# Attention and expert kernel on one core: q, k, v by one 128-partition transfer per tensor and batch, and row scatters no longer ordered among themselves

## The chip, the cores and the metric

The kernel runs on one core of one Trainium2 chip. The metric is device time in microseconds (us): the median of 3 runs is 343.91 us (343.42 to 345.1). One more execution was profiled, and its rows are shown below.

Engines are named as in the profile: PE (matmul), PEld (its weight loads), DVE (VectorE), ACT (ScalarE), POOL (GpSimd), SP (which here only issues loads). Each executes its own instructions in a fixed order, and waits at an instruction until what that one needs is there.

## What is computed

Linear attention over 8 batches of 8 heads, 576 positions and head size 64 gives rows x of 512 numbers, 4608 of them. Each row is then sent to one of 8 experts (512 to 1024 to 512), and its result is scaled by its gate weight.

```python
q_s = exp(q - max(q)) / sum           # over the head size
k_s = exp(k - max(k)) / sum           # over the positions
kv  = einsum('bhsd,bhse->bhde', k_s, v)
x   = einsum('bhsd,bhde->bhse', q_s, kv)   # (4608, 512) after a transpose
logits = x @ w_gate + modality_bias[modality_id]
e_idx, gate_w = argmax(logits), softmax(logits)[e_idx]
out[row] = gate_w * (relu(x[row] @ w1[e]) @ w2[e])   # e = e_idx[row]
```

The kernel first assumes that each of the two modalities has one expert (slot 0 and slot 1, read from the bias on the chip) and computes those two. A loop behind it, `For_i(0, nr)`, does all experts over again for the rows when that assumption fails; in these runs it has no round.

## The kernel before

**Attention, batch by batch.** `load_batch(b)` loads k, v and q (1.18 MB each, fp32) into staging tiles `st`. They come from a pool of 5 buffers, in turn, so that a load waits until the tile five before it has been consumed. `ek` and `eq` (exp on ACT) and `vb` (a cast on POOL, two pieces a batch) are what consumes them. The 576 positions are spread as 64 partitions by 9, so a head fills 64 partitions; the 4 heads 0 to 3 lie on partitions 0 to 63, the heads 4 to 7 on partitions 64 to 127, each half by a transfer of its own.

`stage_a(b)` goes in a chain: `kv_ps` (PE, 36 matmuls), `kinv` and `kvbd` (DVE), `tp_ps` (transposes of `eq`), `et`, `kvT`, `g_ps`, `lg_ps` (PE), then some 30 small DVE operations for logits, the expert and the position of each row (`qi` to `hlo`), and `hv` on POOL. `scl` holds the factors of the rows. `stage_b(b)` makes x in five tiles (`x_ps` on PE, `x_sb` on DVE), sorts the rows by expert with a permutation matmul (`xT_ps`) and writes them on ACT and DVE into `xs`, from the left for slot 0, from the right for slot 1. `id_ps` and `lst` collect where each row goes.

**Experts.** After every second batch, one pass of 512 rows of each slot is complete and `ffn` computes it: 32 matmuls `h_ps`, relu to `hT` (ACT and DVE), 32 matmuls `y_ps`, four copies to `y_sb` (pool `ybuf`, 4 buffers), and for each copy one indirect DMA of POOL that scatters 128 rows of `out`. Eight passes have 512 rows, the last two 384: 608 matmuls, 38 scatters. Three pairs of passes belong to batches 1, 3 and 5; the last four passes (224 matmuls) can begin only after batch 7. The weights of the two slots come by eight 1 MB loads through the same staging tiles and are cast to `W`.

**What sets the order.** A scheduler places the instructions of each engine in one static order, from its own model of dependencies and durations; attention has priority (`high_priority(offset=AHEAD)`), and expert work fills in. It also takes all writes to `out` as one dependency, so each scatter waits for the completion of the one before it. Loads and scatters signal on 8 semaphores each, in turn: a DMA also waits for the one that used its semaphore before.

Of the kernel before, what the change touches and what calls it, by code (L numbers as in the profile page):

```python
# [16 lines left out]
ALU = mybir.AluOpType  # L17
# [3 lines left out]
P = 128  # L21
# [21 lines left out]
def kernel(  # L43
# [12 lines left out]
    nc = tc.nc  # L56
    B, H, S, Dh = q.shape
# [6 lines left out]
    NT = 5  # L64
# [31 lines left out]
    def load_batch(b):  # L96
        for nm, src in (("k", k), ("v", v), ("q", q)):
            t = stage.tile([P, HG, NJ * Dh], FP32, name="st", tag="st")
            for hg in range(2):
                nc.sync.dma_start(  # L100
                    out=t[64 * hg : 64 * hg + 64],
                    in_=bass.AP(
                        tensor=src.tensor,
                        offset=src.offset + (b * H + hg * HG) * S * Dh,
                        ap=[[NJ * Dh, 64], [S * Dh, HG], [1, NJ * Dh]],
                    ),
                )
            st[nm, b] = t
# [6 lines left out]
    wg_f = const.tile([P, KD, E], FP32)  # L115
    nc.scalar.dma_start(out=wg_f, in_=moe_w_gate.rearrange("(kp p) e -> p kp e", p=P))
    mraw = const.tile([P, B, NJ, 2], I32)
# [160 lines left out]
    def stage_a(b):  # L278
# [69 lines left out]
        for t in range(NT):  # L348
# [44 lines left out]
        scl = small.tile([P, NT, H], FP32, name="scl")  # L393
        nc.vector.tensor_tensor(
            out=scl, in0=view(qi, [[H, NT], [1, H]]), in1=view(gsum, [[1, NT], [0, H]]), op=ALU.mult
        )
        na = small.tile([P, NT], FP32, name="na")
# [64 lines left out]
    def stage_b(b):  # L462
# [85 lines left out]

    def ffn(lo, w, slot, ix):
        hT = hbuf.tile([P, KF, GW], BF16, name="hT")  # L550
# [14 lines left out]
        for t in range(w // P):  # L565
            y_ps = ff.tile([P, D], FP32, name="y_ps", tag="ff")
            for kf in range(KF):
                nc.tensor.matmul(  # L568
                    out=y_ps,
                    lhsT=hT[:, kf, t * P : (t + 1) * P],  # L570
                    rhs=W[:, slot, W2 + kf * D : W2 + (kf + 1) * D],
                    start=(kf == 0),
                    stop=(kf == KF - 1),
                )
            y_sb = ybuf.tile([P, D], FP32, name="y_sb")
            if t % 4 < 3:
# [4 lines left out]
            nc.gpsimd.indirect_dma_start(  # L581
                out=out,
                out_offset=bass.IndirectOffsetOnAxis(ap=ix[:, c : c + 1], axis=0),
                in_=y_sb,
                in_offset=None,
                bounds_check=N - 1,
                oob_is_err=False,
            )

    eids = nc.values_load_multi_w_load_instructions(  # L590
        eid_i[0:1, 0:2],
# [6 lines left out]
    for b in range(B):  # L598
# [11 lines left out]
        if b % 2:  # L610
# [8 lines left out]
            for slot, (_, lo, w) in todo:  # L619
                ffn(lo, w, slot, idx)  # L620

# [33 lines left out]
    with tc.For_i(0, nr) as e:  # L655
        kcol = small.tile([P, 1], FP32, name="kcol")
        nc.vector.tensor_copy(out=kcol, in_=view(wrow, [[1, 1]], e))
        sel1 = small.tile([P, NSL], FP32, name="sel1")
# [7 lines left out]
        for _, lo, w in passes_a + passes_b:  # L666
            ffn(lo, w, 0, ixe)

# [29 lines left out]
```

## Time and profile before

| | before |
|---|---|
| median of 3 runs | 343.91 us |
| profiled execution | 346.28 us, span 344.6 us |
| busy: PE, DVE, ACT, POOL | 219.9, 174.6, 116.2, 75.7 us |
| scatters on POOL | 38, busy 37.3 us, idle ahead of them 138.9 us |
| loads of k, v, q | 28.3 MB, issued by SP, 48 transfers |

The span is the time from the first to the last instruction in the profile. Busy time of an engine is an average over stages that have different limits, so the rows further below are taken stage by stage. Durations of matmuls are modelled ends of pipelined work.

### The profile page before, as it was taken

The numbers are of one execution on the slowest core, as the hardware profiler recorded it, in microseconds if no ns is written. First come the engines' busy times: TensorE is split into PE (matmuls) and PEld (weight loads), VectorE is DVE, ScalarE is ACT, GpSimd is POOL, SyncE is SP. The second block draws the span as 40 slices with busy tenths as digits, with TensorE's granted clock in tenths as the row PEclk, the third lists the DMA queues.
The fourth block names the chain that finished last, engine by engine and source line by source line (L and its number), as shares of the span: only waits on it lengthen the run. The fifth ranks groups of instructions, "written<-read, shape, count | busy, mean of one in ns | idle before, by whom it ended". The sixth has DMA issues, their size and how long they took to land.

```text
span 344.6 us, 4646 instructions
## 1 busy us (share of the span) xinstructions
PE 219.9 (64%) x1637; PEld 126.0 (37%) x1657; DVE 174.6 (51%) x558; ACT 116.2 (34%) x161; POOL 75.7 (22%) x86
## 2 busy tenths in 40 slices
PE   0033373369994041572699997499799599999900
PEld 0023262234441031361554553364464334455400
DVE  4056856853520018639649668737858823123210
ACT  0324146144360081242554464332251331422200
POOL 8102100400111125420111433400322322232320
PEclk9999999999999555555589999569999969999985
DMA  7999977963799915999997612100010110212010
GB/s 146 215 222 221 345 233 149 261 242 122 153 233 239 243 70 129 241 208 212 173 213 165 148 55 82 62 1 2 30 60 36 50 71 30 93 61 91 26 69 6
DMA packets 21053, 46.60 MB, mean 135 GB/s; under 512 B 3360, under 2 KB 3360, under 8 KB 21025
## 3 DMA queue, kind: packets, MB, share of 16 engines
q1 hardware_dynamic: 16256, 36.70, 45.8%
q0 software_dynamic: 3040, 9.44, 7.4%
q10 hardware_dynamic: 1728, 0.10, 0.5%
q8 instruction: 15, 0.25, 0.3%
q14 instruction: 14, 0.11, 0.1%
HBM read 36.80 MB, written 9.96 MB: 136 GB/s over the span
## 4 chain that ended last, share of the span: by engine, by line
PE 16%; DMA 13%; issue 13%; DVE 6%; POOL 2%; ACT 1%; POOLq 0%; ACTq 0%
DMA out_dram<-y_sb,idx 13%; PE y_ps L568 5%; PE h_ps L554 4%; PE kv_ps L296 2%; PE xT_ps L494 2%; POOL hv L438 1%; DVE x_sb L486 1%; PE x_ps L478 1%; PE tp_ps L308 1%; PE id_ps L521 1%; ACT ek L284 1%; POOL out_dram L581 0%; PE lg_ps L350 0%; DVE hT L564 0%; DVE y_sb L577 0%
## 5 line engine op out<-in xcount | busy, mean ns | idle before, releaser
L554 PE MATMUL h_ps<-xs,W 128*128 128x512 bf16 (+1 forms) x307 | 76.8, 394 | 3.2 <-ACT xs L504 1.5
L568 PE MATMUL y_ps<-W,hT 128*128 128x512 bf16 x297 | 68.3, 379 | 1.3 <-DVE lo L428 0.7
L581 POOL DMA_INDIRECT out_dram<-y_sb,idx x38 | 37.3, 983 | 138.9 <-DMA out_dram<-y_sb,idx 61.0
L504 ACT CAST xs<-xT_ps 128x512 f32 (+2 forms) x40 | 21.9, 547 | 79.7 <-PE xT_ps L494 76.1
L562 ACT ACTIVATE hT<-h_ps 128x512 bf16<-128x512 f32 (+1 forms) x60 | 34.2, 578 | 39.1 <-PE h_ps L554 31.4
L554 PEld LDWEIGHTS <-W 128*128 128x128 bf16 x320 | 31.8, 103 | 35.7 <-issue 11.2
L568 PEld LDWEIGHTS <-hT 128*128 128x128 bf16 x304 | 29.1, 98 | 33.6 <-DVE hT L564 0.6
L494 PE MATMUL xT_ps<-perm,x_sb 128*128 128x128 bf16 (+1 forms) x160 | 20.8, 260 | 24.8 <-DVE x_sb L486 21.7
L577 DVE COPY y_sb<-y_ps 128x512 f32<-128x512 f32 x30 | 20.5, 687 | 28.2 <-PE y_ps L568 14.8
L486 DVE TENSOR_TENSOR x_sb<-x_ps,scl 128x512 bf16<-128x512 f32 (+1 forms) x40 | 27.4, 686 | 11.0 <-PE x_ps L478 10.8
L564 DVE TENSOR_SCALAR hT<-h_ps 128x512 bf16<-128x512 f32 (+1 forms) x20 | 13.1, 657 | 38.7 <-PE h_ps L554 38.6
L308 PE MATMUL tp_ps<-ident,eq 128*128 128x128 bf16 x144 | 15.5, 282 | 26.2 <-ACT eq L285 21.7
L438 POOL TENSOR_TENSOR hv<-hhi,vals 128x570 bf16<-128x570 bf16 x8 | 12.6, 1578 | 82.4 <-DVE hhi L434 82.4
L296 PE MATMUL kv_ps<-vb,ek 64*128 64x129 bf16 x288 | 18.5, 271 | 16.9 <-POOL vb L287 16.9
L505 DVE CAST xs<-xT_ps 128x512 f32 (+2 forms) x40 | 25.3, 633 | 4.9 <-ACT xs L504 4.6
L287 POOL CAST vb<-st 128x1152 bf16<-128x1152 f32 x16 | 18.6, 1187 | 37.0 <-DMA st<-in_v_dram 29.7
L494 PEld LDWEIGHTS <-x_sb 128*128 128x128 bf16 (+1 forms) x160 | 12.0, 114 | 35.6 <-DVE x_sb L486 31.7
L308 PEld LDWEIGHTS <-eq 128*128 128x128 bf16 x144 | 13.1, 130 | 30.5 <-ACT eq L285 22.4
L478 PE MATMUL x_ps<-kvbd,et 128*128 128x128 bf16 (+1 forms) x160 | 20.9, 271 | 2.7 <-ACT et L318 2.7
L296 PEld LDWEIGHTS <-ek 64*128 64x128 bf16 x288 | 15.7, 116 | 18.6 <-ACT ek L284 13.3
L285 ACT ACTIVATE eq<-st 128x2304 bf16<-128x2304 f32 x8 | 16.9, 2122 | 7.8 <-DMA st<-in_q_dram 7.8
L579 ACT COPY y_sb<-y_ps 128x512 f32<-128x512 f32 x8 | 4.7, 588 | 41.1 <-PE y_ps L568 21.1
(123 smaller groups left out, 210.1 us busy)
## 6 DMA issues: line engine op xcount, KB each, us to landing
st<-in_k_dram SPq DMA_DIRECT2D x16, 576.0 KB, 7.7
st<-in_v_dram SPq DMA_DIRECT2D x16, 576.0 KB, 10.8
st<-in_q_dram SPq DMA_DIRECT2D x16, 576.0 KB, 13.7
st<-in_moe_w_dram SPq DMA_DIRECT2D x8, 1024.0 KB, 12.6
out_dram<-y_sb,idx POOLq DMA_INDIRECT x38, 2.7
mraw<-in_moe_modality_id_dram ACTq DMA_DIRECT2D x2, 36.0 KB, 15.3
bias_b<-n_moe_modality_bias_dram ACTq DMA_DIRECT2D x1, 8.0 KB, 3.0
wg_f<-in_moe_w_gate_dram ACTq DMA_DIRECT2D x1, 16.0 KB
```

Of the source, the lines that this page charges most:

```text
L296: nc.tensor.matmul(out=kv[hg][:, 130 * hp : 130 * hp + 129], lhsT=ek[rows, j, P * hp : P * hp + P], rhs=vb[rows, j, hp, 0:129], start=(j = ...
L308: nc.tensor.transpose(out=view(tp, [[2 * nj * 64, 2], [1, 64]], hp * nj * 64 + jj * 64), in_=eq[:, c0 + jj, P * hp : P * hp + P], identity ...
L478: nc.tensor.matmul(out=x_ps[0:T, P * p_ : P * p_ + P], lhsT=et[:, p_, tcol[t] : tcol[t] + T], rhs=kvbd[:, p_, :], start=True, stop=True,)
L486: nc.vector.tensor_tensor(out=x_sb[0:T], in0=view(x_ps, [[Dh, H], [1, Dh]], 0, (0, T)), in1=view(scl, [[1, H], [0, Dh]], t * H, (0, T)), o ...
L494: nc.tensor.matmul(out=xT_ps[:, kd, 0:T], lhsT=view(x_sb, [[1, P]], kd * P, (0, T)), rhs=perm[0:T, t, 0:T], start=True, stop=True,)
L504: wa = nc.scalar.copy(out=window(a, passes_a[ph], T, ph == NPH - 1), in_=xT_ps[:, :, 0:T])
L505: wb = nc.vector.tensor_copy(out=window(a + right, passes_b[ph], T, ph == NPH - 1, True), in_=xT_ps[:, :, 0:T])
L554: nc.tensor.matmul(out=h_ps[:, 0:w], lhsT=W[:, slot, kd * F + f * P : kd * F + (f + 1) * P], rhs=xs[:, kd, lo : lo + w], start=(kd == 0), ...
L562: nc.scalar.activation(out=hT[:, f, 0:w], in_=h_ps[:, 0:w], func=ACT.Relu)
L568: nc.tensor.matmul(out=y_ps, lhsT=hT[:, kf, t * P : (t + 1) * P], rhs=W[:, slot, W2 + kf * D : W2 + (kf + 1) * D], start=(kf == 0), stop=( ...
L577: nc.vector.tensor_copy(out=y_sb, in_=y_ps)
L581: nc.gpsimd.indirect_dma_start(out=out, out_offset=bass.IndirectOffsetOnAxis(ap=ix[:, c : c + 1], axis=0), in_=y_sb, in_offset=None, bound ...
```

## The change

Each of k, v and q is loaded by one transfer over 128 partitions: even heads on partitions 0 to 63, odd heads on 64 to 127. What follows from the other order of heads: the gate weights `wg_f` come in four transfers instead of one, `scl` is written by two operations of half the size, and `x_ps` is written with the columns of the heads in their places. Scatters are declared independent of each other; only the loop behind waits for them.

```diff
-            for hg in range(2):
-                nc.sync.dma_start(
-                    out=t[64 * hg : 64 * hg + 64],
-                        offset=src.offset + (b * H + hg * HG) * S * Dh,
-                        ap=[[NJ * Dh, 64], [S * Dh, HG], [1, NJ * Dh]],
+            nc.sync.dma_start(
+                out=t,
+                    offset=src.offset + b * H * S * Dh,
+                    ap=[[NJ * Dh, P], [2 * S * Dh, HG], [1, NJ * Dh]],
...
-    nc.scalar.dma_start(out=wg_f, in_=moe_w_gate.rearrange("(kp p) e -> p kp e", p=P))
+    for h2 in range(2):
+        for hl in range(2):
+            nc.scalar.dma_start(
+                out=wg_f[64 * h2 : 64 * h2 + 64, 2 * hl : 2 * hl + 2, :],
...
+        for hl in range(2):
+            nc.vector.tensor_tensor(
+                out=view(scl, [[H, NT], [2, HG]], hl),
+                in0=view(qi, [[H, NT], [1, HG]], HG * hl),
...
-                    out=x_ps[0:T, P * p_ : P * p_ + P],
+                    out=view(x_ps, [[2 * Dh, 2], [1, Dh]], (4 * (p_ % 2) + p_ // 2) * Dh, (0, T)),
...
-            nc.gpsimd.indirect_dma_start(
+            store = nc.gpsimd.indirect_dma_start(
...
+            tc.declare_no_dep(store.ins, group=stores, reason="rows of their own")
+            tc.add_to_no_dep_group(stores, store.ins)
+            if stores == "stores":
+                stored.append(store)
...
+        for before in stored:
+            tc.add_manual_dep(first.ins, before.ins.name, ...)
```

The order of the built programs shows three places where instructions move.

**SP, start of the program.** SP's first loads of batch 0 and 1 before; DMAHW is a semaphore of a load, and "waits" names what must have landed first.

```order
L100 DMA st<-in_k_dram 64x4x576 x2
L100 DMA st<-in_v_dram 64x4x576 x2
L100 DMA st<-in_q_dram 64x4x576 [waits DMAHW0_49]
L100 DMA st<-in_q_dram 64x4x576 [waits DMAHW1_49]
L100 DMA st<-in_k_dram 64x4x576 [waits DMAHW2_49]
L100 DMA st<-in_k_dram 64x4x576 [waits DMAHW3_49]
```

And of the changed kernel, the same loads:

```order
L100 DMA st<-in_k_dram 128x4x576
L100 DMA st<-in_v_dram 128x4x576 [waits DMAHW0_49]
L100 DMA st<-in_q_dram 128x4x576 [waits DMAHW1_49]
L100 DMA st<-in_k_dram 128x4x576 [waits DMAHW2_49]
L100 DMA st<-in_v_dram 128x4x576 [waits DMAHW3_49]
L100 DMA st<-in_q_dram 128x4x576 [waits DMAHW4_49,Activation_49]
```

One row stands for two. The semaphores 0 to 3 belonged to `bias_b`, `wg_f` and the two `mraw` transfers; now they belong to `bias_b` and the first three of `wg_f`, so that v waits for `bias_b`, and the second k no longer for `mraw`.

**ACT, around batch 2.** Before, behind `ek` of batch 2: `hT` are the relus of the expert passes, `ek` here is that of batch 3, `eq` those of batches 2 and 3, and `et` belongs to the chain of batch 2.

```order
L562 ACTIVATE hT<-h_ps 128x512 x6
L272 CAST W<-st 128x2048
L579 COPY y_sb<-y_ps 128x512
L272 CAST W<-st 128x2048
L562 ACTIVATE hT<-h_ps 128x512 x6
L284 ACTIVATE ek<-st 128x4x9x64
L579 COPY y_sb<-y_ps 128x512
L285 ACTIVATE eq<-st 128x4x9x64 x2
L318 COPY et_180<-tp_ps 128x4x256
```

The changed kernel from `et` of batch 2 on; `eq` here is that of batch 3, `ek` that of batch 4, `kvT` and `lg` belong to batch 2:

```order
L328 COPY et_180<-tp_ps 128x4x256
L328 COPY et_180<-tp_ps 128x4x64
L349 COPY kvT<-kvT_ps 128x512
L576 ACTIVATE hT<-h_ps 128x512 x4
L295 ACTIVATE eq<-st 128x4x9x64
L387 ACTIVATE lg<-lg 128x40
L576 ACTIVATE hT<-h_ps 128x512
L294 ACTIVATE ek<-st 128x4x9x64
L481 TENSOR_LOAD aoff_i
```

Before, both expert passes of the first pair, with their 12 relus and the copies to `y_sb`, stood ahead of `eq` and `et` of batch 2; now `eq` of batch 2 stands in batch 1, and the relus are spread over batches 2 and 3, behind `et`. PE's order moved in the same way: before, 128 expert matmuls between batch 1 and the transposes of batch 2, now 49 to 73 in every batch from 2 to 7.

**POOL, the first scatters.** Before; DMASW is a semaphore of a scatter, `vb_183` is v of batch 3.

```order
L581 DMA out_dram<-y_sb,idx 4608x512 [waits DVE_49]
L581 DMA out_dram<-y_sb,idx 4608x512 [waits DMASW0_49,DVE_49]
L581 DMA out_dram<-y_sb,idx 4608x512 [waits DMASW1_49,DVE_49]
L581 DMA out_dram<-y_sb,idx 4608x512 [waits DMASW2_49,Activation_49]
L581 DMA out_dram<-y_sb,idx 4608x512 [waits DMASW3_49,DVE_49]
L581 DMA out_dram<-y_sb,idx 4608x512 [waits DMASW4_49,DVE_49]
L581 DMA out_dram<-y_sb,idx 4608x512 [waits DMASW5_49,DVE_49]
L287 CAST vb_183<-st 128x2x9x64 [waits DMAHW0_49,DMAHW7_49,PE_49,Pool_49]
```

And of the changed kernel, where `vb_183` is now v of batch 5:

```order
L452 TENSOR_TENSOR hv<-hhi,vals 128x570 [waits DVE_49]
L297 CAST vb_182<-st 128x2x9x64 [waits PE_49,Pool_49]
L595 DMA out_dram<-y_sb,idx 4608x512 [waits DVE_49] x3
L297 CAST vb_183<-st 128x2x9x64 [waits DMAHW7_49,PE_49,Pool_49]
L297 CAST vb_183<-st 128x2x9x64 [waits PE_49,Pool_49]
L595 DMA out_dram<-y_sb,idx 4608x512 [waits Activation_49]
```

The wait of each scatter for the one before it is gone (from the ninth on, one waits for the eighth before it), and the casts of `vb` for batches 3 and 4 stand ahead of the first scatter instead of behind the seventh and eighth.

## Rows read from the trace of the kernel before

**Rows 1.** Page, part 2: busy tenths in 40 slices of 8.6 us.
```profile
PE   0033373369994041572699997499799599999900
PEclk9999999999999555555589999569999969999985
DMA  7999977963799915999997612100010110212010
```

**Rows 2.** Windows: busy us of each engine, then PEclk, DMA share, GB/s.
```profile
22.00:34.00 12.00, 4.38 (x50) 3.37 (x50) 8.49 (x33) 5.05 (x5) 2.10 (x2) 1.00 1.05 221
38.00:46.00 8.00, 3.91 (x32) 2.79 (x29) 5.39 (x13) 2.02 (x5) 1.65 (x1) 1.00 1.03 393
```

**Rows 3.** Timeline, batches 0 and 1: start us, us, engine, instruction, [idle before <-releaser].
```profile
14.66 0.18 DVE L183 CAST modf<-mraw 64x32 f32<-64x32 int32 x1 [6.54 <-DMA mraw<-in_moe_modality_id_dram]
20.13 0.18 DVE L183 CAST modf<-mraw 64x32 f32<-64x32 int32 x1 [5.29 <-DMA mraw<-in_moe_modality_id_dram]
21.13 2.12 ACT L285 ACTIVATE eq<-st 128x2304 bf16<-128x2304 f32 x1 [7.85 <-DMA st<-in_q_dram]
26.25 0.21 DVE L322 TENSOR_SCALAR kinv<-kv_ps 128x2 f32<-128x2 f32 x2
...
49.27 0.26 DVE L322 TENSOR_SCALAR kinv<-kv_ps 128x2 f32<-128x2 f32 x2 [2.27 <-PE kv_ps L296]
```

**Rows 4.** Timeline of POOL: `hv` of batches 0 to 7.
```profile
40.56 1.65 POOL L438 TENSOR_TENSOR hv<-hhi,vals 128x570 bf16<-128x570 bf16 x1 [6.41 <-DVE hhi L434]
64.89 1.66 POOL L438 TENSOR_TENSOR hv<-hhi,vals 128x570 bf16<-128x570 bf16 x1 [22.68 <-DVE hhi L434]
137.64 1.14 POOL L438 TENSOR_TENSOR hv<-hhi,vals 128x570 bf16<-128x570 bf16 x1 [2.69 <-DVE hhi L434]
163.14 1.65 POOL L438 TENSOR_TENSOR hv<-hhi,vals 128x570 bf16<-128x570 bf16 x1 [11.18 <-DVE hhi L434]
188.23 1.66 POOL L438 TENSOR_TENSOR hv<-hhi,vals 128x570 bf16<-128x570 bf16 x1 [15.02 <-DVE hhi L434]
217.02 1.65 POOL L438 TENSOR_TENSOR hv<-hhi,vals 128x570 bf16<-128x570 bf16 x1 [0.35 <-DVE hhi L434]
243.71 1.64 POOL L438 TENSOR_TENSOR hv<-hhi,vals 128x570 bf16<-128x570 bf16 x1 [22.73 <-DVE hhi L434]
268.42 1.58 POOL L438 TENSOR_TENSOR hv<-hhi,vals 128x570 bf16<-128x570 bf16 x1 [1.38 <-DVE hhi L434]
```

**Rows 5.** Timeline between the first pair of expert passes and batch 2.
```profile
115.64 0.69 DVE L577 COPY y_sb<-y_ps 128x512 f32<-128x512 f32 x1 [9.03 <-DMA out_dram<-y_sb,idx]
116.29 0.97 POOL L581 DMA_INDIRECT out_dram<-y_sb,idx  x1 [8.75 <-DMA out_dram<-y_sb,idx]
121.82 0.59 ACT L579 COPY y_sb<-y_ps 128x512 f32<-128x512 f32 x1 [19.99 <-DMA out_dram<-y_sb,idx]
122.30 4.14 ACT L285 ACTIVATE eq<-st 128x2304 bf16<-128x2304 f32 x2
124.48 2.10 PE L308 MATMUL tp_ps<-ident,eq 128*128 128x128 bf16 x18 [17.53 <-ACT eq L285]
```

**Rows 6.** Windows: batch 7's period, and two us behind 176; columns as in rows 2.
```profile
243.71:268.42 24.71, 23.42 (x202) 12.70 (x203) 18.45 (x60) 8.23 (x15) 6.53 (x6) 1.00 0.15 55
176.00:178.00 2.00, 2.00 (x20) 1.12 (x17) 0.00 (x0) 1.83 (x4) 0.00 (x0) 1.00 1.04 200
```

**Rows 7.** Timeline of the end of the program.
```profile
327.10 0.17 PE L629 MATMUL n_ps<-cnt_b,ones 128*128 128x1 bf16 x1
327.30 0.69 DVE L577 COPY y_sb<-y_ps 128x512 f32<-128x512 f32 x1 [1.03 <-PE n_ps L629]
333.85 0.97 POOL L581 DMA_INDIRECT out_dram<-y_sb,idx  x1 [3.15 <-DMA out_dram<-y_sb,idx]
```

**Rows 8.** Timeline of PE: expert matmuls at two rates.
```profile
75.56 4.79 PE L554 MATMUL h_ps<-xs,W 128*128 128x512 bf16 x11 [0.22 <-issue]
285.62 7.07 PE L568 MATMUL y_ps<-W,hT 128*128 128x512 bf16 x32
```

More of the change, by code (lines that the diff above doesn't have):

```diff
@@ L98, in load_batch @@
             t = stage.tile([P, HG, NJ * Dh], FP32, name="st", tag="st")
-            for hg in range(2):
-                nc.sync.dma_start(
-                    out=t[64 * hg : 64 * hg + 64],
-                    in_=bass.AP(
-                        tensor=src.tensor,
-                        offset=src.offset + (b * H + hg * HG) * S * Dh,
-                        ap=[[NJ * Dh, 64], [S * Dh, HG], [1, NJ * Dh]],
-                    ),
-                )
+            nc.sync.dma_start(
+                out=t,
+                in_=bass.AP(
+                    tensor=src.tensor,
+                    offset=src.offset + b * H * S * Dh,
+                    ap=[[NJ * Dh, P], [2 * S * Dh, HG], [1, NJ * Dh]],
+                ),
+            )
             st[nm, b] = t
@@ L115 @@
     wg_f = const.tile([P, KD, E], FP32)
-    nc.scalar.dma_start(out=wg_f, in_=moe_w_gate.rearrange("(kp p) e -> p kp e", p=P))
+    for h2 in range(2):
+        for hl in range(2):
+            nc.scalar.dma_start(
+                out=wg_f[64 * h2 : 64 * h2 + 64, 2 * hl : 2 * hl + 2, :],
+                in_=bass.AP(
+                    tensor=moe_w_gate.tensor,
+                    offset=moe_w_gate.offset + (2 * h2 + hl) * Dh * E,
+                    ap=[[E, Dh], [4 * Dh * E, 2], [1, E]],
+                ),
+            )
     mraw = const.tile([P, B, NJ, 2], I32)
@@ L393, in stage_a @@
         scl = small.tile([P, NT, H], FP32, name="scl")
-        nc.vector.tensor_tensor(
-            out=scl, in0=view(qi, [[H, NT], [1, H]]), in1=view(gsum, [[1, NT], [0, H]]), op=ALU.mult
-        )
+        for hl in range(2):
+            nc.vector.tensor_tensor(
+                out=view(scl, [[H, NT], [2, HG]], hl),
+                in0=view(qi, [[H, NT], [1, HG]], HG * hl),
+                in1=view(gsum, [[1, NT], [0, HG]]),
+                op=ALU.mult,
+            )
         na = small.tile([P, NT], FP32, name="na")
@@ L547, with ffn @@
     W2 = KD * F
-    def ffn(lo, w, slot, ix):
+    def ffn(lo, w, slot, ix, stores):
         hT = hbuf.tile([P, KF, GW], BF16, name="hT")
@@ L588, in ffn @@
             )
+            tc.declare_no_dep(store.ins, group=stores, reason="rows of their own")
+            tc.add_to_no_dep_group(stores, store.ins)
+            if stores == "stores":
+                stored.append(store)
+    stored = []
     eids = nc.values_load_multi_w_load_instructions(
@@ L619 @@
             for slot, (_, lo, w) in todo:
-                ffn(lo, w, slot, idx)
+                ffn(lo, w, slot, idx, "stores")
     pl = ctx.enter_context(tc.tile_pool(name="plan", bufs=1))
@@ L656 @@
         kcol = small.tile([P, 1], FP32, name="kcol")
-        nc.vector.tensor_copy(out=kcol, in_=view(wrow, [[1, 1]], e))
+        first = nc.vector.tensor_copy(out=kcol, in_=view(wrow, [[1, 1]], e))
+        for before in stored:
+            tc.add_manual_dep(
+                first.ins,
+                before.ins.name,
+                mybir.DependencyInfo(mybir.DependencyClass.Sync, mybir.DependencyReason.DATA),
+                reason="rows are stored again",
+            )
         sel1 = small.tile([P, NSL], FP32, name="sel1")
@@ L666 @@
         for _, lo, w in passes_a + passes_b:
-            ffn(lo, w, 0, ixe)
+            ffn(lo, w, 0, ixe, "stores again")
 _INS = ['q', 'k', 'v', 'moe_modality_id', 'moe_w_gate', 'moe_modality_bias', 'moe_w1', 'moe_w2']
```

## Prediction

> **What bounds the kernel now.** I read the page's slices first [rows 1]. The DMA engines are 90% busy or more through most of the first 190 us and nearly idle after; PE is below half busy there except around 75 to 105 us, and full only from 276 us on; the granted clock is at 0.5 between about 110 and 175 us. So there are three stages with different limits: a first half with loads, a middle, and a tail of PE alone.
>
> Next the windows tell what the busy DMA engines move [rows 2]. From 22 to 34 us only q, k and v are under way, by transfers over 64 partitions: 221 GB/s at a full DMA share. From 38 to 46 us it is the weights, over 128 partitions: 393 GB/s at the same share. Busy does not mean fast here.
>
> The clock of the program is `hv`, the last step of a batch's chain [rows 4]. Batch 0 has it at 40.56 us; the periods after it are 24.33, 72.75, 25.50, 25.09, 28.79, 26.69 and 24.71 us. Seven periods would be alike, and one is 48 us too long: it contains the first pair of expert passes and a stall. In the stall [rows 5] DVE and ACT stand at copies to `y_sb` because no buffer is free; a buffer is free only when its scatter has landed, each scatter waits for the one before it, and beside the loads one takes some 9.7 us (8.75 us of waiting and 0.97 of issue). ACT waits 19.99 us at one copy, `eq` of batch 2 stands behind it in ACT's order, and PE's transposes behind that: 17.53 us idle. The loads cannot be what is missing there: when the copy is done, two `eq` start back to back.
>
> Behind `hv` of batch 7, the last four passes end PE at 327.27 us, that is 58.85 us later [rows 4, 7]. Then 17.33 us pass to the end of the span: the last copy is made at 327.99, but its scatter is issued only at 333.85, at the end of the queue of scatters, and the program ends 10.75 us after that.
>
> **The change, part by part.** My sum goes along the chain of `hv`.
>
> *Start.* `eq` of batch 0 waits for q until 21.13 us, but `kinv` starts only at 26.25: DVE is held at `modf` by the two small `mraw` transfers, until 14.66 and 20.13 us, and does 6.1 us of preparation behind the second one [rows 3]. Those transfers share the DMA engines with the loads; each took its 5.5 us and more while the loads ran at 221 GB/s. If they advance in step with the loads, 20.13 becomes 2 + 18.1 x 221/393 = 12.2 us; if the loads do not matter to them, it stays at 20.13, plus about 1.3 us for three more issues ahead of them on ACT, an estimate: 21.4. I take 15, nearer to the first, since the DMA share is full in that stretch and a shared engine is the nearest explanation. In the changed order some of the preparation stands ahead of the second `modf`, about 0.6 us, so `kinv` starts at 20.5. From `kinv` to `hv` batch 0 takes 14.3 us [rows 3, 4], which is DVE's and PE's own work; `hv` at 34.8. SP's v now waits for `bias_b`, and later loads for pieces of `wg_f`; that holds back v by 2 us or so, hidden since `kv_ps` has until 20 us. Gain: 5.8 us, bounds -0.6 and 8.6.
>
> *Batch 1.* 24.33 us, a chain in which no load is waited for; kept. `hv` of batch 1 at 59.1.
>
> *Batches 2 to 7.* Here both parts act. The scatters issue without their wait, so copies find buffers; and the static order is another one: expert matmuls are spread, 54, 70, 49, 73, 67 and 60 in the six periods, where before 128 stood in a block in one. The nearest row for such a period is batch 7's [rows 6]: 24.71 us with 202 matmuls, of which 129 are attention's, so 73 of the experts, at the full clock and with no load running; PE is 23.42 us busy. Batches 2 and 3 without any expert work, at the lower clock, have 25.5 and 25.1 between them and their followers, batch 5, at the full clock with the most expert work, 28.79. Both the chain of small operations and PE's sum therefore land near 25. I take 25.0 for each of the six: 150 us, where the old periods sum to 203.5. Lower bound 23.0: the shortest stretch seen from `kinv` to `hv` (14.3 us) and the 8.7 from batch 0's `hv` to batch 1's `kinv` at 49.27 [rows 3]. Upper bound 28.8, batch 5's. Loads need 3.54 MB a batch: 9 us at 393 GB/s, 16 at 221, both under 25, so in this region their rate is covered by the period; their cover goes only when the period falls below 16. Gain: 53.5 us, bounds 30.7 and 65.5.
>
> *New work.* One more DVE operation a batch for `scl`, 0.2 us by the small operations of [rows 3]; counted inside the 25.0. `x_ps` has its columns elsewhere, the same matmuls.
>
> *The tail.* 58.85 us from the last `hv` to PE's end, kept: it is matmuls, 7.07 us for 32 [rows 8]. The last scatter is then issued some 0.2 us behind its copy, at 328.2 on the old clock in place of 333.85, and the 10.75 us behind it stay: gain 5.6 us. One copy arrives every 1.8 us (a quarter of 7.07) and a scatter costs POOL 0.97, so no queue builds up.
>
> Sum: 34.8 + 24.3 + 150 + 58.9 + 11.7 (0.9 for copy and issue, 10.75 behind it) = 279.7 us of span, 65 below 344.6. The profiled execution took 346.28, 1.7 over its span, and the median of the runs is 2.4 below it: 279.7 + 1.7 - 2.4 = 279 us.
>
> **A rule against the trace.** [Rows 2] give 221 against 393 GB/s for transfers over 64 and 128 partitions. The Trainium skill (SBUF — State Buffer, "Door 1: The DMA port swizzle") says that 64 partitions in a row reach only 8 of 16 ports, 218 GB/s against 436; the trace agrees on the first, and stays below the second. The skill's DMA: Bandwidth & Descriptors, "Rules for kernel authors", says of two transfers to partition halves that both already use all 16 engines and merely serialize; read alone, that leaves nothing to win in rate, which is the first rival.
>
> **The rivals.**
> *The loads stay at 221 GB/s.* What limits them could be their 2.3 KB pieces, which stay; the weights have 4 and 2 KB pieces, and the 393 GB/s window holds both, which speaks against it. Then the start gains nothing, and the rest stays, as 16 us a batch fit: 279 + 6 = 285.
>
> *The spread order stalls on POOL.* POOL executes scatters, casts of v and `hv` in one order. `hv` of batch 2 now stands behind a cast of batch 4's v, and scatters stand behind each `hv`. If this holds all six periods at batch 5's 28.8: 279 + 23 = 302. Against it: POOL is busy for 6.53 of the 24.71 us of batch 7's period, with five scatters in it [rows 6].
>
> *The clock stays low: slower.* A matmul of the experts takes 0.435 us at one level and 0.221 at the other [rows 8], 1.2 and 2.4 GHz; the granted clock fell to 0.5 in the long stall and was back by 176 us, within batch 4's period, the first that has expert work spread through it [rows 1, 4, 6]. If spread work leaves PE too many gaps, 62 expert matmuls cost 13.3 us more in a batch, of which 1.3 hide in PE's idle time: 12 a batch. All six and the tail's first passes at that level would be over 279 + 72 = 351. It decides from five and a half of six batches on, as 65/12 shows. Against it: PE would be 23 of 25 us busy. The Trainium skill (TensorE: Matmul & The Clock Gate, "HAM oscillation") warns of just such waits between pieces of work.
>
> *Shorter chains.* With all operands early, the periods could be 23.0: 279 - 12 = 267.
>
> **How the numbers follow.** Forecast 0.62 (its own range 268 to 291: start and periods within 1.5 us), loads at the old rate 0.08, POOL 0.13, clock 0.03, short chains 0.14. The likeliest is 279. From 263 (short periods and the start's best) to 300 at most 2 in 10 are left out: half of POOL's case, the clock's, a corner of the last. A change of 0.5% (1.7 us) is what this measurement can tell from none. Only the clock's case gives slower: faster 0.97, same 0.01, slower 0.02.
>
> **What would show it.** In the profile after: windows with k, v, q alone near 390 GB/s; `kinv` of batch 0 near 20 us; eight `hv` 23 to 27 us apart with no 70 us gap; no copy to `y_sb` waiting for a scatter for more than some us; granted clock 1.00 from batch 2 on; the last scatter within 1 us of the last copy. I am wrong if a period exceeds 30 us, if `mraw` still lands at 20 us, or if PE's clock falls between 100 and 200 us.

## The result, and the profile after

The changed kernel takes 285.69 us (median of 4 runs, 284.43 to 288.24) against 344.49 for the kernel before: a ratio of 0.8305, 95% interval 0.8243 to 0.8368. The forecast was 279 with a range of 263 to 300. The profiled execution took 284.43 us with a span of 282.7. Some executions of a kernel are slow ones, among them one of e3 below at 564.03 us and one of e4 at 304.33, so the ratios compare fast runs alone.

The page's slices of the kernel after (7.07 us each; same rows as [rows 1], and what the DMA engines moved):

```profile
PE   0044358236998999787897979889997799999910
PEclk9999999999999999999999899999999999999985
DMA  5999999969959996143030002101201203021020
GB/s 166 329 392 405 387 390 400 363 205 330 319 202 332 344 377 265 39 140 141 0 151 0 0 3 111 39 1 43 108 2 44 104 37 114 37 111 66 2 87 5
```

Most loads are done after some 115 us; the last is issued at 124.21 us, where the kernel before issued its last three from 183.66 on. PE is 70% busy or more in every slice from 70 us to its end, and its granted clock shows no stretch at 0.5 until then. A window with loads of k, v and q, columns as in [rows 2], and SP's first load of weights, which sets the window's end:

```profile
10.00:22.00 12.00, 4.36 (x55) 3.89 (x56) 10.90 (x37) 5.07 (x4) 4.64 (x5) 1.00 1.05 394
...
20.53 1.05 SPq L263 DMA_DIRECT2D st<-in_moe_w_dram  x2
```

394 GB/s at a full share, where the kernel before had 221. (From 22 to 34 us, the window of [rows 2], this kernel already moves mostly weights.) The timeline of POOL has the clock of the program, `hv` of batches 0 to 7 (answers to [rows 4]):

```profile
32.38 1.65 POOL L452 TENSOR_TENSOR hv<-hhi,vals 128x570 bf16<-128x570 bf16 x1 [8.33 <-DVE hhi L448]
58.84 1.14 POOL L452 TENSOR_TENSOR hv<-hhi,vals 128x570 bf16<-128x570 bf16 x1 [13.69 <-DVE hhi L448]
87.96 1.65 POOL L452 TENSOR_TENSOR hv<-hhi,vals 128x570 bf16<-128x570 bf16 x1 [11.47 <-DVE hhi L448]
112.32 1.65 POOL L452 TENSOR_TENSOR hv<-hhi,vals 128x570 bf16<-128x570 bf16 x1 [10.62 <-DVE hhi L448]
136.90 1.65 POOL L452 TENSOR_TENSOR hv<-hhi,vals 128x570 bf16<-128x570 bf16 x1 [7.90 <-DVE hhi L448]
163.90 1.65 POOL L452 TENSOR_TENSOR hv<-hhi,vals 128x570 bf16<-128x570 bf16 x1 [15.16 <-DVE hhi L448]
188.95 1.65 POOL L452 TENSOR_TENSOR hv<-hhi,vals 128x570 bf16<-128x570 bf16 x1 [10.52 <-DVE hhi L448]
212.24 1.58 POOL L452 TENSOR_TENSOR hv<-hhi,vals 128x570 bf16<-128x570 bf16 x1 [12.37 <-DVE hhi L448]
```

The periods are 26.46, 29.12, 24.36, 24.58, 27.00, 25.05 and 23.29 us. The one of 72.75 us is gone. At the start, on DVE (answers to [rows 3]):

```profile
9.94 0.17 DVE L193 CAST modf<-mraw 64x32 f32<-64x32 int32 x1
10.69 0.18 DVE L193 CAST modf<-mraw 64x32 f32<-64x32 int32 x1
13.91 3.32 DVE L151 TENSOR_SCALAR wrow<-iota_i 128x8 f32<-128x8 int32 x1
19.54 0.21 DVE L332 TENSOR_SCALAR kinv<-kv_ps 128x2 f32<-128x2 f32 x2
```

`modf` waits for nothing now, and the preparation behind it holds one operation of 3.32 us on 8 columns. At the end (answers to [rows 7]) the last scatter follows its copy at once, and 12.1 us follow it, to 282.7:

```profile
269.44 0.17 PE L649 MATMUL n_ps<-cnt_b,ones 128*128 128x1 bf16 x1
269.64 0.69 DVE L591 COPY y_sb<-y_ps 128x512 f32<-128x512 f32 x1 [1.03 <-PE n_ps L649]
270.61 0.98 POOL L595 DMA_INDIRECT out_dram<-y_sb,idx  x1 [0.75 <-DVE okm L667]
```

The forecast's sum looks confirmed. The experiments ask whether its reasons are.

### The profile page after: what moved, and what is told of

Read it like the earlier page. It is cut to its first block, busy times and chain, and to the rows that moved or that the text cites. A ratio compares the mean times of both kernels' runs of the same rounds, so it can differ in the third digit from the quotient of the medians.

```text
span 282.7 us, 4628 instructions
## 1 busy us (share of the span) xinstructions
PE 208.1 (74%) x1657; PEld 116.2 (41%) x1657; DVE 174.7 (62%) x566; ACT 115.8 (41%) x161; POOL 75.3 (27%) x86
## 4 chain that ended last, share of the span: by engine, by line
PE 34%; issue 23%; DVE 6%; POOL 6%; ACT 4%; DMA 2%; POOLq 0%; DVEq 0%; ACTq 0%
PE y_ps L582 15%; PE h_ps L568 10%; POOL hv L452 3%; PE xT_ps L508 2%; PE kv_ps L306 2%; DVE xs L519 2%; DMA st<-in_v_dram 2%; POOL out_dram L595 2%; ACT xs L518 1%; ACT et L328 1%; PE tp_ps L318 1%; DVE x_sb L500 1%; PE x_ps L492 1%; PE id_ps L535 1%; DVE y_sb L591 1%
## 5 line engine op out<-in xcount | busy, mean ns | idle before, releaser
L568 PE MATMUL h_ps<-xs,W 128*128 128x512 bf16 (+1 forms) x320 | 76.0, 378 | 1.7 <-ACT xs L518 0.7
L582 PE MATMUL y_ps<-W,hT 128*128 128x512 bf16 x304 | 73.2, 379 | 1.7 <-DVE y_sb L591 1.1
L568 PEld LDWEIGHTS <-W 128*128 128x128 bf16 x320 | 30.3, 99 | 29.7 <-issue 4.4
L508 PE MATMUL xT_ps<-perm,x_sb 128*128 128x128 bf16 (+1 forms) x160 | 19.0, 234 | 14.6 <-DVE x_sb L500 14.6
L508 PEld LDWEIGHTS <-x_sb 128*128 128x128 bf16 (+1 forms) x160 | 11.0, 104 | 27.3 <-DVE x_sb L500 22.6
L306 PEld LDWEIGHTS <-ek 64*128 64x128 bf16 x288 | 14.8, 110 | 15.7 <-ACT ek L294 10.9
L294 ACT ACTIVATE ek<-st 128x2304 bf16<-128x2304 f32 x8 | 17.0, 2124 | 6.2 <-PE kv_ps L306 3.7
L492 PE MATMUL x_ps<-kvbd,et 128*128 128x128 bf16 (+1 forms) x160 | 18.1, 244 | 1.5 <-ACT et L328 1.5
L318 PE MATMUL tp_ps<-ident,eq 128*128 128x128 bf16 x144 | 14.4, 253 | 5.3 <-DVE et L326 2.7
L318 PEld LDWEIGHTS <-eq 128*128 128x128 bf16 x144 | 11.5, 115 | 10.8 <-issue 6.3
```

Source lines behind the costliest of these rows:

```text
L306: nc.tensor.matmul(out=kv[hg][:, 130 * hp : 130 * hp + 129], lhsT=ek[rows, j, P * hp : P * hp + P], rhs=vb[rows, j, hp, 0:129], start=(j = ...
L318: nc.tensor.transpose(out=view(tp, [[2 * nj * 64, 2], [1, 64]], hp * nj * 64 + jj * 64), in_=eq[:, c0 + jj, P * hp : P * hp + P], identity ...
L508: nc.tensor.matmul(out=xT_ps[:, kd, 0:T], lhsT=view(x_sb, [[1, P]], kd * P, (0, T)), rhs=perm[0:T, t, 0:T], start=True, stop=True,)
L568: nc.tensor.matmul(out=h_ps[:, 0:w], lhsT=W[:, slot, kd * F + f * P : kd * F + (f + 1) * P], rhs=xs[:, kd, lo : lo + w], start=(kd == 0), ...
L582: nc.tensor.matmul(out=y_ps, lhsT=hT[:, kf, t * P : (t + 1) * P], rhs=W[:, slot, W2 + kf * D : W2 + (kf + 1) * D], start=(kf == 0), stop=( ...
```

## The experiments

All were timed in 3 rounds (the last in 5) beside the kernel before, at 344.9 to 345.9 us. "Block" is the number of expert matmuls that PE's written order has ahead of `id_ps` of batch 2 and between that and `id_ps` of batch 3 (the forecast's 54 and 70 were cut at other rows; over the six periods both lists sum to 373). "b0" is `hv` of batch 0, "b2" the period of batch 2, in the profiled execution.

| kernel | us | ratio to before, interval | block | b0 | b2 |
|---|---|---|---|---|---|
| before | 344.49 | 1 | 128, 0 | 40.56 | 72.75 |
| e10 before, loads in order | 331.72 | 0.9598 (0.9547 to 0.9649) | 106, 22 | 40.85 | 52.74 |
| e6 halves, second pass held back | 327.78 | 0.9492 (0.9453 to 0.9531) | 64, 64 | 39.10 | 56.96 |
| e2 independent scatters alone | 326.23 | 0.9454 (0.9393 to 0.9516) | 128, 0 | 40.90 | 58.42 |
| e3 after, with half transfers | 323.89 | 0.9356 (0.9274 to 0.9439) | 128, 0 | 39.59 | 58.70 |
| e11 e6, loads in order | 315.47 | 0.9135 (0.9089 to 0.9181) | 64, 64 | 39.61 | 36.95 |
| e5 after, block written | 313.56 | 0.9087 (0.9029 to 0.9144) | 128, 0 | 32.45 | 58.21 |
| e9 e3, loads in order | 304.50 | 0.8810 (0.8756 to 0.8864) | 103, 25 | 39.34 | 37.41 |
| e4 gate pieces on POOL | 303.19 | 0.8732 (0.8637 to 0.8828) | 46, 70 | 40.38 | 29.70 |
| e1 loads alone | 294.81 | 0.8543 (0.8461 to 0.8624) | 46, 70 | 32.08 | 29.20 |
| e8 one expert's weights | 291.75 | 0.8454 (0.8418 to 0.8491) | 53, 75 | 32.16 | 30.90 |
| e12 start in order | 291.71 | 0.8449 (0.8410 to 0.8487) | 46, 70 | 37.19 | 28.17 |
| after | 285.69 | 0.8305 (0.8243 to 0.8368) | 46, 70 | 32.38 | 29.12 |
| e7 preparation first | 284.89 | 0.8249 (0.8213 to 0.8284) | 46, 70 | 31.62 | 29.38 |

### One part of the change at a time

**e1**, the kernel after without the lines that make the scatters independent:

```
-            tc.declare_no_dep(store.ins, group=stores, reason="rows of their own")
-            tc.add_to_no_dep_group(stores, store.ins)
-            if stores == "stores":
-                stored.append(store)
```

> The loads of the changed kernel, and the scatters ordered among themselves again. PE's written order here is that of the changed kernel: the expert matmuls stand spread over the periods, not in one block of 128. Theory of the prediction (the ordered scatters make the stall, wherever the matmuls stand): a scatter waits for the one before it, some 9.7 us each beside loads as in the kernel before, eight belong to the first pair of passes and four buffers take the first four, so four copies wait some 10 us each: 285.7 + 40 = 326 us, between 315 and 335, with copies to y_sb waiting for a scatter and one period between two hv of over 50 us. Rival (the written order carries the gain: spread matmuls give each scatter the time it needs): 285.7 + 5.6 for the queue of scatters at the end = 291 us, all periods under 31 us.

**e2**, the kernel before with these four lines added (and the dependence of the later loop on the scatters).

> The loads of the kernel before, and the scatters independent. PE's written order here is that of the kernel before: 128 expert matmuls in one block between the hv of batch 1 and that of batch 2. Theory of the prediction: without the wait the stall of 48 us and the 5.6 us at the end are gone and only the start's gain is missing, 285.7 + 8 (hv of batch 0 at 40.56 in place of 32.38) = 294 us, no period over 32 us. Rival (the order matters too): the block of 128 matmuls at 0.22 to 0.44 us stands on the chain, 28 to 56 us more in that period; these matmuls are then missing in later periods, but those do not fall under 24 us: 294 + 28 = 322 us, between 312 and 345.

**e3**, the kernel after with

```
+            for hl in range(2):
+                nc.sync.dma_start(
+                    out=t[64 * hl : 64 * hl + 64],
...
+                        offset=src.offset + (b * H + hl) * S * Dh,
+                        ap=[[NJ * Dh, 64], [2 * S * Dh, HG], [1, NJ * Dh]],
```

> The changed kernel, with each tensor of a batch loaded by two transfers of 64 partitions again, one for each head parity; the scatters stay independent. Bytes, pieces and places in memory are those of the changed kernel. PE's written order falls back to one block of 128 expert matmuls ahead of hv of batch 2, as in the kernel before. On the rate: if partitions decide, the windows with loads alone show 221 GB/s as in the kernel before; if the layout or the number of queues decides, 394 as in the changed kernel. On the time: theory of the prediction, 285.7 + 6 to 8 for the start = 293 us; rival, the block of matmuls on the chain, 322 us, as in the kernel with independent scatters alone.

Both expectations from the forecast's theory failed. With ordered scatters and the new loads there is no stall: 294.81 us, every period under 31, the rival's 291. With independent scatters and the old loads a period of 58.42 us stays: 326.23, the rival's 322, and e3 repeats it. So the loads' part alone, with the written order that comes with it, gives 50 us of the 59, the scatters' part alone 19. e3 settles the rate; its window with loads alone:

```profile
22.00:34.00 12.00, 4.26 (x52) 3.58 (x52) 5.54 (x21) 5.93 (x6) 0.99 (x1) 1.00 1.05 214
```

214 GB/s with the layout of the change and two queued halves, 394 with one transfer: what counts is the partitions of one transfer. A fixed cost of each transfer is not what halves the rate: by the trace's records of DMA packets the same pieces of 2304 bytes take 185 ns each in e3 (median, 10 to 34 us) and 95 in the kernel after (10 to 20 us), and in e3 no more than 0.07 us pass between one start and the next. The Trainium skill (SBUF — State Buffer, "Can I just issue two DMAs to hit both halves?") says that two such transfers serialize and only one over all 128 partitions reaches all ports; the trace agrees.

What the ordered scatters cost in e1 is 4.7 us in batch 3's period, and more at the end (18.8 us from `n_ps` to the end, 13.3 in the kernel after). The timeline of POOL and DVE in e1:

```profile
101.52 0.98 POOL L595 DMA_INDIRECT out_dram<-y_sb,idx  x1 [7.49 <-DMA out_dram<-y_sb,idx]
...
106.02 2.80 DVE L386 TENSOR_TENSOR lg<-lg,mx 128x40 f32<-128x40 f32 x1
...
106.52 1.17 POOL L297 CAST vb<-st 128x1152 bf16<-128x1152 f32 x1
```

POOL's cast of v stands behind three of the scatters, 9.7 us later than in the kernel after (96.79), and falls on `lg`, a step of batch 3's chain that takes 0.20 us elsewhere. No copy to `y_sb` waits for a scatter.

### Is it the block of matmuls?

The written order differs with the loads: one block of 128 expert matmuls, or 46 and 70. Two kernels set it apart from the loads. **e5**, the kernel after with

```
+            with tc.high_priority(offset=2 * AHEAD if ph == 0 else 0):
                 for slot, (_, lo, w) in todo:
                     ffn(lo, w, slot, idx, "stores")
```

> The changed kernel, loads and independent scatters kept, with the first pair of expert passes written ahead of batch 2's work: 128 expert matmuls in one block ahead of hv of batch 2, then 0, 46, 64, 63 and 72. If the written order carries the gain (what the two halves of the change showed so far): the period of batch 2 goes from 29 to about 58 us, as in the kernel with independent scatters alone, batch 3's does not fall below 24, and the time is 285.7 + 29 = 315 us, between 306 and 325. If the rate of the loads carries it, wherever the matmuls stand: 285.7 us, at most 290.

**e6**, e3 with the second pass of the first pair emitted behind batch 2 and each of its `h_ps` matmuls tied, for the order alone, to `id_ps` of batch 2:

```
+            for m in mms[n0:]:
+                tc.add_manual_dep(m.ins, ids[-1].ins.name,
+                    mybir.DependencyInfo(mybir.DependencyClass.NoSync, mybir.DependencyReason.SCHED_ONLY), ...)
```

> The loads by two transfers of 64 partitions (214 GB/s), scatters independent, and the second pass of the first pair held behind hv of batch 2 in PE's written order: 64 and 64 expert matmuls in the periods of batches 2 and 3 in place of 128 and 0. If the written order carries the gain: 64 matmuls at 0.44 us leave the period of batch 2, 28 us, and batch 3's grows by 3 to 4: 323.9 - 28 + 3.5 = 299 us, between 291 and 306. If the slow loads themselves hold batch 2 back: 320 us or more, with waits of POOL or ACT for k, q or v in that period.

e5 came as the order theory said, 313.56 us. Its `eq` of batch 2 is made at 81.84 us, and PE is full of the block until the first transposes are through; timeline of ACT and DVE:

```profile
81.84 2.11 ACT L295 ACTIVATE eq<-st 128x2304 bf16<-128x2304 f32 x1
...
103.38 0.69 DVE L326 COPY et<-tp_ps 128x1024 bf16<-128x1024 bf16 x1 [1.48 <-PE tp_ps L318]
```

PE is busy for 21.43 of the 21.54 us between them, at the full clock. So a block can cost this much where all operands are there. In e6 the period stayed at 56.96, and the time, 327.78, was no better than e3's: there the order is not the cause. Its windows (columns as in [rows 2]) show a hole that the block had only filled:

```profile
90.00:96.00 6.00, 0.00 (x0) 0.00 (x0) 0.00 (x0) 2.28 (x2) 1.56 (x2) 0.77 1.03 302
96.00:102.00 6.00, 0.00 (x0) 0.00 (x0) 0.00 (x0) 0.00 (x0) 2.23 (x2) 0.50 1.05 277
```

The timeline of ACT and PE has what ended it:

```profile
104.26 2.12 ACT L296 ACTIVATE eq<-st 128x2304 bf16<-128x2304 f32 x1 [9.58 <-DMA st<-in_q_dram]
106.43 2.10 PE L319 MATMUL tp_ps<-ident,eq 128*128 128x128 bf16 x18 [16.90 <-ACT eq L296]
```

PE and DVE stand still, DMA is full, and `eq` of batch 2 waits for q. Why q of batch 2 is so late shows on SP, in the kernel before already. Its timeline of SP:

```profile
57.54 0.59 SPq L100 DMA_DIRECT2D st<-in_q_dram  x1
58.38 6.08 SPq L253 DMA_DIRECT2D st<-in_moe_w_dram  x2
73.11 1.00 SPq L262 DMA_DIRECT2D st<-in_moe_w_dram  x2
87.27 1.66 SPq L100 DMA_DIRECT2D st<-in_k_dram  x2
91.15 1.26 SPq L100 DMA_DIRECT2D st<-in_v_dram  x2
95.04 1.92 SPq L100 DMA_DIRECT2D st<-in_q_dram  x3
```

One half of q of batch 2 is issued at 57.54 us, the other among the three from 95.04 on, behind the second expert's weights and behind k and v of batch 3: the written order of SP had split the pair. It is the second of the three, issued at 95.67 us, by the semaphore that `eq` of batch 2 waits for, and by that semaphore it landed at 107.4 us, 14.4 us before the copy in [rows 5] at which the forecast's stall ends. In e2, with SP's order the same, that half is issued at 95.59 and landed at 108.25, and ACT has

```profile
108.34 2.12 ACT L285 ACTIVATE eq<-st 128x2304 bf16<-128x2304 f32 x1 [0.81 <-DMA st<-in_q_dram]
```

One transfer per tensor has no second half to leave behind.

### The late half of q

**e9** is e3, **e10** the kernel before and **e11** is e6, each with the loads on SP tied to one another in the program's order, for the order alone:

```
+    def in_order(d):
+        if row:
+            tc.add_manual_dep(d.ins, row[-1].ins.name,
+                mybir.DependencyInfo(mybir.DependencyClass.NoSync, mybir.DependencyReason.SCHED_ONLY), ...)
+        row.append(d)
```

> Loads by two transfers of 64 partitions (214 GB/s), scatters independent, and all loads on SP written in the program's order. In the half-transfer kernels so far SP's written order has the second half of q of batch 2 behind the second expert's weights and behind k and v of batch 3, and ACT waited for it until 104 us. PE's written order follows by itself: 103 and 25 expert matmuls in the periods of batches 2 and 3, in place of 128 and 0. Theory (the late half of q held batch 2; the block beside it only filled the time): no engine waits for q in batch 2's period, eq of batch 2 before 85 us, and the period is 29 us and the price of 57 more expert matmuls, 29 x 57 / 82 = 20 by the block kernel: 49 in place of 58.7, batch 3's 2 more, 323.9 - 8 = 316 us, between 308 and 319. Rival (the low rate holds it): a wait for k, q or v of over 5 us stays in that period, 321 us or more.

> The kernel before, its scatters still ordered among themselves, with all loads on SP written in the program's order, and nothing else changed. PE's written order follows: 106 and 22 expert matmuls in the periods of batches 2 and 3. Theory of the prediction (the ordered scatters make the stall; the late half of q lies hidden behind it): the copies still wait some 10 us each for scatters beside the loads, and the time falls by 10 us at most: 335 to 345 us. Rival (the late half of q is the stall's root, the scatters only add to it): the period of batch 2 falls from 72.75 to 50 us or less, 322 us, between 315 and 332.

> Loads by two transfers of 64 partitions, scatters independent, loads on SP in the program's order, and the second pass of the first pair held behind hv of batch 2: 64 and 64 expert matmuls in the periods of batches 2 and 3. It takes both suspects of the 58 us period away and keeps the rate at 214 GB/s. Theory: the period of batch 2 is 29 us and 18 more expert matmuls at 0.35 us, 35 us, batch 3's 28: 327.8 - 22 - 3 = 303 us, between 296 and 308. Rival (the low rate holds it): waits for k, q or v of over 5 us in that period, 318 us or more.

e9 is 304.5 us, 19.4 below e3: on SP nothing but the place of the second halves has moved, PE's written order has followed, and the period of batch 2 falls from 58.70 to 37.41 us. The timeline has `eq` of batch 2 at

```profile
82.46 2.12 ACT L311 ACTIVATE eq<-st 128x2304 bf16<-128x2304 f32 x1
```

without a wait, as expected; the price of the 57 more expert matmuls was expected at 20 us, and the period is 8.3 above the kernel after's (37.41 - 29.12). e10 fell between its two theories, 331.72 us. With q in order `eq` of batch 2 no longer stands behind ACT's stalled copy and runs at 85.20 us (122.30 before). What is left is POOL's order: `hhi` of batch 2 is made by 104.42 us, and `hv` stands behind scatters that wait 17.4 us in that period, 8.7 at once. The timeline of POOL in e10:

```profile
107.25 0.97 POOL L596 DMA_INDIRECT out_dram<-y_sb,idx  x1 [8.70 <-DMA out_dram<-y_sb,idx]
116.94 0.98 POOL L596 DMA_INDIRECT out_dram<-y_sb,idx  x1 [8.71 <-DMA out_dram<-y_sb,idx]
117.93 1.16 POOL L453 TENSOR_TENSOR hv<-hhi,vals 128x570 bf16<-128x570 bf16 x1
```

e11's period, 36.95, came near the expected 35, its time did not (315.47 for 303): the next two periods are 31.59 and 32.56 us. It also shows that the 8.3 us of e9 are no price by the number of matmuls in the period: with 39 fewer of them the period is the same within 0.5 us. Both kernels have 44 expert matmuls ahead of the first transpose of batch 2 and start the transposes 22.3 us behind `hv` of batch 1; the kernel after has one ahead and starts them after 13.6. Holding the pass back costs 11 us against e9. The rival's wait for k, q or v is in batch 2's period of neither.

So two things kept batch 2 back side by side. The half of q alone is worth 13.9 us (e10), the scatters alone 18.9 (345.49 times 1 - 0.9454), and both, with the layout, 41 (e9): more than their sum, since with one gone the other still holds the batch (`eq` at 108.34 in e2, `hv` at 117.93 in e10). The last 18.8 us, from e9 to the kernel after, are the rate with what PE's order makes of it: by the two profiles, whose spans are 20.1 us apart, 7.0 us at the start, -2.9 in batch 1, 8.3 in batch 2, 7.0 in batches 3 to 7 and 0.8 behind.

### The start, and the second expert's weights

**e4** issues the four pieces of `wg_f` from POOL:

```
-            nc.scalar.dma_start(
+            nc.gpsimd.dma_start(
                 out=wg_f[64 * h2 : 64 * h2 + 64, 2 * hl : 2 * hl + 2, :],
```

> The changed kernel, with the four pieces of wg_f issued by POOL in place of ACT, so that v, q of batch 0 and k, v of batch 1 no longer wait for a small transfer before they are issued. Theory: in the changed kernel the start is set by v of batch 0, issued only at 6.11 us behind bias_b; issued at 1.3 us it gives kv_ps and kinv 4 us earlier and hv of batch 0 at 28.5 in place of 32.38: 285.7 - 4 = 281.7 us if the rest of the chain follows. Rival: kinv stands behind DVE's preparation (13.5 to 19.5 us), which waits for POOL's iota and fills, and these now stand behind the cast of v on POOL: kinv stays at 19 to 20 us and the time at 285.7, within 1.5 us.

It is 17.5 us slower than the kernel after. v was issued at 1.30 us and its cast still started at 12.22 (12.77 after): the loads share the rate, and an earlier issue bought nothing. But the cast now stands ahead of POOL's iotas and fills, and DVE pays:

```profile
16.04 5.03 DVE L196 CAST modf<-mraw 64x8 f32<-64x8 int32 x1
...
16.69 4.21 POOL L247 MEMSET xs<- 128x2432 f32 x2
...
27.56 0.21 DVE L332 TENSOR_SCALAR kinv<-kv_ps 128x2 f32<-128x2 f32 x2
```

The second `modf` on `mraw` also started only at 15.84 us, when that transfer had landed (10.69 in the kernel after). `kinv` came 8 us later, and the granted clock is 0.50 from there to `hv` of batch 1. The window of batch 1's period:

```profile
40.38:67.17 26.79, 13.70 (x131) 11.02 (x129) 18.12 (x59) 12.39 (x14) 4.88 (x4) 0.50 0.98 344
```

The rest of the loss lies in periods 0.3 to 3 us longer than after's and 2 us behind the last `hv`; why those at a clock of 0.93 and more are longer was not settled.

**e7** ties everything on DVE that waits for a small transfer behind the conversions of the iota tiles (`early`), for the order alone:

```
+    for y in gates:
+        for x in early:
+            tc.add_manual_dep(y.ins, x.ins.name,
+                mybir.DependencyInfo(mybir.DependencyClass.NoSync, mybir.DependencyReason.SCHED_ONLY), ...)
```

> The changed kernel, with DVE's small conversions of the iota tiles written ahead of everything on DVE that waits for a small transfer (in the changed kernel they run at 13.5 to 17.4 us, beside POOL's cast of v and its fill, at 2 to 3 us each in place of 0.2). If this preparation sets the start: kinv of batch 0 starts when kv_ps is done, at 16.3 in place of 19.54 us, hv at 29.1 in place of 32.38, and the time is 285.7 - 3.3 = 282.4 us. Rival (what follows is set by loads and weights, so the start is given back by batch 2): hv of batch 0 at 29, of batch 2 at 88 as before, 285.7 us within 1.

284.89 us: not to be told from the kernel after. The profiled execution is the slowest of its five, 287.17 us. Timeline of e7, DVE and ACT:

```profile
7.51 0.16 DVE L152 TENSOR_SCALAR wrow<-iota_i 128x8 f32<-128x8 int32 x1
...
16.17 0.23 DVE L341 TENSOR_SCALAR kinv<-kv_ps 128x2 f32<-128x2 f32 x2 [2.29 <-PE kv_ps L315]
...
16.18 2.12 ACT L304 ACTIVATE eq<-st 128x2304 bf16<-128x2304 f32 x1 [5.28 <-DMA st<-in_q_dram]
```

`kinv` is 3.4 us earlier, as expected, but q lands at 16.18 us and `hv` of batch 0 is only 0.8 earlier; by batch 2 even that is 0.5. **e12** is e7 with the pieces of `wg_f` on POOL behind its iotas, so that v and q are issued at once, with the first casts of v behind those pieces, and with k of batch 1 waiting for q of batch 0:

```
+            if (nm, b) == ("k", 1):
+                after(d, q0[0], mybir.DependencyClass.Sync, mybir.DependencyReason.DATA)
```

> The changed kernel with its start put in order: DVE's conversions of the iota tiles ahead of everything that waits for a small transfer, the four pieces of wg_f issued by POOL behind its iotas (so v and q of batch 0 are issued at once), and k of batch 1 issued only when q of batch 0 has landed. With the conversions alone, kinv started 3.4 us earlier but the transposes then waited for eq, whose q landed at 16 us, and hv of batch 0 came only 0.8 us earlier. If q is that next wait: three tensors of 1.18 MB at 394 GB/s are 9 us, so q lands at 12 to 13 us, hv of batch 0 comes at 28.5 to 29.5 in place of 32.38, and the time is 285.7 - 3.3 = 282.4 us. Rival (the start is not what later periods wait for, or the time goes to the delayed k of batch 1): hv of batch 2 no earlier than 87 us, and 285.7 us within 1.5.

291.71 us, a miss: with k, v and q alone of the large loads in flight q landed hardly earlier (`eq` at 15.48, 15.75 in the kernel after). The expectation had 394 GB/s from the start; the windows show 166 from 2 to 6 us, at a DMA share of 0.65, 353 from 6 to 10 and 281 from 10 to 15.5. Why they begin so low is open. The second `modf` waited for `mraw` until 15.64 us and then took 3.25 us beside POOL's two fills, and `kinv` came at 21.56. Of 4.8 us lost at `hv` of batch 0, 1.2 were left at `hv` of batch 1. No version here beats the kernel after by more than can be told.

**e8** leaves out the second expert's weights (both sides use the first's):

```
-                load_weights(eids[1], 1, (nc.scalar, nc.vector))
...
-                ffn(lo, w, slot, idx, "stores")
+                ffn(lo, w, 0, idx, "stores")
```

> The changed kernel without the weights of the second expert: they are neither loaded nor cast, and both sides use the first expert's (this part of the computation is left out). The number of matmuls is the same, the written order nearly (53, 75, 49, 67, 65, 64). If the casts of the second expert's weights on ACT and DVE (4 of 1.2 to 1.9 us, between the small steps of batches 1 and 2) and their 4 MB of loads stretch those two periods: 26.5 and 29.1 become 24.5 and 25.5, and the time 285.7 - 5.6 = 280 us. Rival (a period with 46 or more expert matmuls behind a cold chain is that long by itself): both periods stay within 1 us and the time at 285.7.

Both theories missed: 291.75 us, with 30.90 and 29.53 us for batches 2 and 3 (29.12 and 24.36 after) although four casts and 4 MB are gone. PE's order has 12 more expert matmuls in those two. So taking the casts and their loads away did not shorten the periods; since the written order moved with them, what they cost by themselves is not shown, and what stretches the periods is open.

## Why the prediction was right, and where its reasons were not

The time is 6.7 us above the forecast. By its own terms, for the span: start 32.38 (34.8 forecast), batch 1 26.46 (24.3), batches 2 to 7 153.4 (150), the last `hv` to PE's end 57.4 (58.9), the end 13.1 (11.7): 282.7 against 279.7, so 3.0 of the 6.7. The other 3.7 are the step from the profiled time to the median: the forecast took off 2.4, as the median before lay that far below the profiled execution, and here the profiled execution was the lowest of four, 1.3 below the median.

**Batches 2 to 7: right in size, wrong in cause.** "The loads cannot be what is missing there" is the step that failed. The two `eq` back to back in [rows 5] showed only that q had landed by 122 us, not that it had been there all the time, and SP's rows, which show when it was issued, were not read. The second half of q of batch 2 landed at 107.4, and e2 shows that it ends a period of 58.42 us by itself. Hence the second failed step, "in this region their rate is covered by the period", worked out from bytes (16 us a batch): it leaves out where in the queue a transfer stands. The forecast credited the scatters with the stall and the order of PE with the rest; e2 and e10 show that neither the scatters nor the order of the loads alone gives half. That the 150 us came out is luck as far as the cause goes: by the forecast's reasons e2 and e3 would have had them too, at 294 and 293 us, and they took 326.23 and 323.89.

**The rival "the loads stay at 221 GB/s"** was priced at 285 us. It did not occur, but e3 has it: 323.89, and 304.5 with the halves in order. The forecast would have been off by 20 to 40 us where it felt safe. That the rate itself rises was right, and so was the weighing of the Trainium skill's port rule (SBUF — State Buffer, "Door 1: The DMA port swizzle") above the row that two halves merely serialize: both hold, 214 GB/s for the halves and 394 for the whole.

**The start: right within 2.4 us, by another path.** Of the 2.4 us, 1.0 are `kinv` (19.54 for 20.5) and 1.5 the chain behind it (12.84 for 14.3). `mraw` was ready at 9.94 and 10.69 us, under the lower bound of 12.2, though not because the loads are faster: e3 has `kinv` at 19.77 with loads at 214 GB/s, since v and q are issued behind the small transfers (v at 7.01 us there), and its `modf` at 10.46 and 11.22. In e4 and e12, where v and q are issued at once at the full rate, the second `modf` waits for `mraw` until 15.84 and 15.64. But e3's `hv` of batch 0 is at 39.59: q sets it. The hold of v by `bias_b`, forecast at 2 us and hidden, is 3.9 (v issued at 6.11 us, 2.26 before), and e4 shows that it costs 0.55 us at the cast of v (12.77 to 12.22).

**Batch 1** was 2.1 us longer than kept, **batch 2** 4.1 longer than 25; neither cause was found (e8 has 26.47 and 30.90 us without the second expert's weights). The other five sum to 124.3 for 125. Of the two old periods that the forecast calls free of expert work, 25.50 and 25.09 us, the second holds 50 expert matmuls, by PE's weight loads; as a witness for 25 us it still stands.

**Tail and end.** The scatters' queue is gone as forecast; e1 gives 5.5 us for it at the end (18.8 - 13.3), forecast 5.6. The 12.1 us behind the last scatter were 10.75 before. The passes have 624 expert matmuls, 320 `h_ps` and 304 `y_ps` on the page, 240 of them in the last four passes, and not 608 and 224; the 58.85 us were taken from the trace and don't hang on it.

**The other rivals.** POOL's order did not hold all six periods at 28.8 (it held batch 2's in e10, with ordered scatters). The clock stayed at 0.94 and above in all periods. Shorter chains came in one, 23.29.

## What to carry to other kernels

Ahead of saying what a stall waits for, ask of each operand behind it when its transfer was issued, and what stands ahead of it in that queue: an operand that is there at the end of a stall may have come in the middle of it. Two waits that lie side by side give little when removed singly and their joint worth together, so each part of a change is costed with the other still in place as well. A tensor that one consumer needs whole is best loaded by one transfer: halves took the rate here from 394 to 214 GB/s, and the written order could put other loads between them (19.4 us).

## What the runs showed of the hardware

Small DVE operations stand still while POOL casts or fills: `wrow` took 3.32 us after POOL's cast of v had begun and 0.16 in e7, ahead of it; `lg` 2.80 for 0.20 in e1, beside a cast of v; `modf` 5.03 in e4 for 0.16 in the kernel after, beside fills of 4.21. `kinv`, which reads PSUM, ran in 0.23 us at 16.17 in e7 beside a fill. The Trainium skill (SBUF — State Buffer, "Who interferes with whom") states that DVE, in some of its forms, and GpSimd hold a shared pair of ports exclusively for a whole instruction, and that whoever issues second fully blocks. The trace agrees that DVE stands for the whole of POOL's instructions; which of the two came first it does not settle, as `lg` starts 0.50 us ahead of the cast by the records. So an engine's move in time costs, not only its length: in e1 the 9.7 us by which the cast came later reached the chain as 2.6 us of DVE.
